# Where K and Q are rounded, when PSUM is evacuated, and which queue loads an index: eight edits to an attention and MLP kernel

## The chip, the core and the metric

The kernel runs on one core of a Trainium2 chip. The metric is device time in microseconds, as the median of several runs; one further execution was recorded by the hardware profiler. TensorE (PE), VectorE (DVE), ScalarE (ACT), GpSimd (POOL) and SyncE (SP) each take their own instructions in program order. DMAs are issued from SP, ACT or POOL.

## The reference

```python
# q, k, v: (8, 8, 576, 64) float32; global_idx: 8 positions
mask = (abs(i - j) <= 32) | is_global[i] | is_global[j]
attn = softmax(where(mask, q @ k.T / 8, -1e9))
x = (attn @ v) rearranged to (8 * 576, 512)
out = (s * relu(x @ w_in) ** 2 + b) @ w_out      # w_in 512x2048, w_out 2048x512
```

Every query sees a window of 32 positions on both sides and the 8 global positions. A global query sees all 576 keys.

## The kernel before, in words

**Pairs.** The 64 heads are worked as 32 pairs `p`, two heads at a time, four pairs to a batch (`bi, hp = divmod(p, 4)`). A pair has five chunks of 120 keys with the 8 global keys placed ahead of each, so that Q and K tiles have five blocks of 128 columns. For each chunk, `qk` (L482) makes one matmul into PSUM tile `pss` (pool `ps_s`, two buffers), ScalarE takes the exponential (`e`, L488) and VectorE multiplies by the mask (`em`, L491). In the next pair, `pv` (L501) multiplies by V and by ones into `po`. `norm_steps` (L519) then makes two ScalarE steps, `ln` (L541) and `rep` (L544), and VectorE writes the row `xt` (L547) of the MLP's input. `scatter` (L555) copies the results of global queries to their places in `xt`: eight GpSimd copies whose column is a register, `greg_p`, loaded at L808 from the index tile `gidx_i64`.

**Q and K of a pair.** Pairs 0 to 7 are loaded by GpSimd in bf16, six rows to a partition (`load_kq`, L152), and turned by TensorE transposes (`trans`, L437; `trans_a` for K, `trans_b` for Q). K is evacuated by VectorE (L457), Q by ScalarE for one head and then VectorE for the other (L473). Pairs from 8 on are loaded by SP in float32 (`load_nat`, L160) into rings `nat` of four, rounded to bf16 into `natb` of two (`round_nat`, L181), by ScalarE or, from p > 8 in pairs with hp 1 and 2, by GpSimd. K is then turned by a DMA transpose on SP (`turn_k`, L187), and Q by TensorE (`turn_q`, L193); VectorE places Q (L204). `put_kq` (L426) adds the global keys and queries by two small VectorE copies (L428, L432). V goes through a ring `vring` of four: `cast_v` rounds it on ScalarE (up to pair 7) or GpSimd, `put_v` (L419) adds the global values, by VectorE up to pair 7 and by a DMA on SP after that.

**MLP.** `moe_quanta` (L566) cuts the MLP into pieces of four TensorE matmuls: the first layer into `psh` (L581) with ReLU on ScalarE (`r`, L588) and the square on VectorE (`g`, L591); the second layer into `pso` (L596), then a VectorE evacuation (L607 or L610) and a store on SP. Evacuations of the first output rows wait for a bias row and are finished later by `release` (L840). From pair 5 on a pair has eight slots and takes about one quantum in each. By the order of the quanta, pairs with hp 1 and 2 carry the first layer and pairs with hp 3 and 0 the second.

**Order.** It is written by hand; the program is recorded in that order on each engine. `first_pair` (L708) runs slots 0 to 4 of pairs 0 to 4, without the MLP; `run_pair` (L640) runs slots 5 to 7 of pair 4 and all slots of the pairs after it. In a slot, the functions in `later` that the slot before left are run (`prev`), after the slot's own TensorE work; an evacuation that is appended to `later` so comes one slot after its matmuls:

```python
        for s in range(8) if p > 4 else range(NCH, 8):
            prev, later[:] = list(later), []
...
            for f in prev:
                f()
...
            for f in extra.get(s, ()):
                f()
            Q(nq[s])
```

A table `ex` (L868 to L902) gives each pair its extra work by slot: rounding at slots 5 and 7, `turn_k` and `put_v` at 7, `turn_q` at 5. Loads for pair `p + 4` are issued at the head of pair `p` (L856). A memset of eight elements (L855) at pair 5 lets SP start the loads of pair 8 only then.

Of the kernel before, what the change touches and what calls it, by code (L numbers as in the profile page):

```python
# [16 lines left out]
P = 128  # L17
# [49 lines left out]
def kernel(  # L67
# [45 lines left out]

    nat = {t: const.tile([P, NV, NCH, 2, D], FP32, name=f"nat{t}", tag=f"nat{t}") for t in "kq"}
    natb = {
        t: const.tile([P, 2, NCH * P], BF16, name=f"natb{t}", tag=f"natb{t}") for t in "kq"
    }

    xt = const.tile([P, 4, NX * S + 2 * HB * NCH - S], BF16)
# [16 lines left out]
            tensor=global_idx.tensor, offset=global_idx.offset, ap=[[0, P // NG], [1, NG], [1, 1]]  # L136
        ),
    )
    nc.sync.dma_start(out=gidx_i64[:], in_=_bcast_dram(global_idx[:], P))
    vring = const.tile([P, NV, NCH, 2, D], BF16)  # L140
    qbufs = [const.tile([P, 2, LQ], BF16, name=f"qbd{i}", tag=f"qbd{i}") for i in range(3)]
    gqd = [const.tile([P, 2, D], BF16, name=f"gqd{i}", tag=f"gqd{i}") for i in range(2)]
# [35 lines left out]

    kts = {}

    def round_nat(eng, t, p):  # L181
        eng(
            out=natb[t][0:KC, p % 2].rearrange("p (c h d) -> p c h d", c=NCH, h=2),
            in_=nat[t][0:KC, p % NV],
        )

    def turn_k(p):  # L187
        kts[p] = kqp.tile([P, KT0 + NCH * P], BF16, tag="kt", name="kt")
        nc.sync.dma_start_transpose(
            out=kts[p][:, KT0:].rearrange("p (c x) -> p c x", x=P), in_=natb["k"][:, p % 2]  # L190
        )

    def turn_q(p):  # L193
        ps = ps_s.tile([P, LQ], BF16, tag="s", name="pst")
        for c in range(NCH):
            nc.tensor.transpose(  # L196
                ps[:, P * c : P * c + P], natb["q"][:, p % 2, P * c : P * c + P], ident[:]
            )

        def place():  # L200
            ktile[p] = kts[p][:, KT0 - NG : KT0 - NG + LQ]
            for hh in range(2):
                r = slice(D * hh, D * hh + D)
                nc.vector.tensor_copy(  # L204
                    out=view(qbufs[p % 3][r, hh], [P, NCH], [HB + NG, 2], [1, HB]),
                    in_=view(ps[r], [P, NCH], [HB, 2], [1, HB]),
                )
            put_kq(p)

        later.append(place)  # L210

    def load_v(eng, p):
        load_nat(eng, "v", p)
# [221 lines left out]
        )  # L435

    def trans(t, p):  # L437
        if p < 5:
            ps = ps_m.tile([P, LQ], BF16, tag="moe", name="pst")
        else:  # L440
            ps = ps_s.tile([P, LQ], BF16, tag="s", name="pst")
        for j in range(NJ):
            n = N6 if j == NJ - 1 else NP6
            for hh in range(2):
                nc.tensor.transpose(
                    ps[D * hh : D * hh + D, NP6 * j : NP6 * j + n],
                    six[t][:n, p % NR, hh, j], ident[:n, :n],
                )
        return ps

    def trans_a(p, later=later):
        ps = trans("k", p)
        kt = ktp.tile([P, LQ], BF16, tag="kt", name="kt")
        ktile[p] = kt[:]

        def evac():
            nc.vector.tensor_copy(  # L457
                out=view(kt[:, NG:], [P, NCH], [NJ, KC // NJ], [1, NJ]),
                in_=view(ps[:], [KC // NJ, NCH], [1, KC // NJ], [NP6, NJ]),
            )  # L460
            if p >= 5:
                put_kq(p)

        later.append(evac)

    def trans_b(p, later=later):
        ps = trans("q", p)

        def evac():
            n = HB // NJ  # L470
            for hh, eng in ((1, nc.scalar.copy), (0, nc.vector.tensor_copy)):
                r = slice(D * hh, D * hh + D)
                eng(  # L473
                    out=view(qbufs[p % 3][r, hh], [P, NCH], [HB + NG, 2], [NJ, n], [1, NJ]),
                    in_=view(ps[r], [2 * n, NCH], [n, 2], [1, n], [NP6, NJ]),
                )
            if 1 < p < 5:
                put_kq(p)

        later.append(evac)  # L480

# [155 lines left out]

    A, V, G = nc.scalar.copy, nc.vector.tensor_copy, nc.gpsimd.tensor_copy

    def run_pair(p, nq, extra):  # L640

        bi, hp = divmod(p, 4)
        if hp == 0 and p > 4:
            open_batch(bi)
        for s in range(8) if p > 4 else range(NCH, 8):
            prev, later[:] = list(later), []
            if s < NCH:
                qk(p, s)
                if s in (1, 2):
                    step()  # L650
                if s == 4 and hp == 0 and bi > 1:
                    later.append(lambda: scatter(bi - 1))
                if s == 2 and p + 1 < NSIX:
                    cast_v(A, p + 1)
                if s == 2 and NSIX <= p + 2 < NPAIR:
                    cast_v(G, p + 2)
            elif s == 5:
                if p == 4:
                    cast_v(A, 5)
                if p + 1 < NSIX:  # L660
                    trans_b(p + 1)
            elif s == 6 and p + 1 < NSIX:
                trans_a(p + 1)
            for f in prev:
                f()
            if s == 0:
                pv(p - 1)
                pending.extend(norm_steps(p - 1))
            if s == 6 and p + 1 < NSIX:
                put_v(V, p + 1)  # L670
            for f in extra.get(s, ()):
                f()
            Q(nq[s])
# [34 lines left out]
    def first_pair(p, extra={}):  # L708
# [5 lines left out]
        for s in range(NCH):  # L714
            prev, later[:] = list(later), []
            now = []
            if p or s > 1:
                warm(1, bank)
            qk(p, s)
            if s in (1, 2):  # L720
                if p < 4:
                    (trans_a, trans_b)[s - 1](p + 1, now)
                if p:

                    pv(p - 1, (2 - s,))
                    if s == 1:
                        pending.extend(norm_steps(p - 1))
            elif s == 3:
                step()
            elif s == 4 and p == 3:  # L730
                cast_v(A, 4)
# [3 lines left out]
                f()  # L735
            if s == 1:
                step()
            if s == 0 and p == 4:
                put_v(V, 4)

# [12 lines left out]
    clear(qbufs[1][0:D, 1], LQ)  # L753
    clear(qbufs[1][D:P, 0], LQ)
    select_first()
    warm(3)
    vkey = const.tile([P, NCH], FP32)
    nc.vector.tensor_scalar(
# [20 lines left out]
    def clear_q2():  # L779
# [2 lines left out]

    first_pair(0, {
        1: [lambda: cast_v(A, 0), lambda: build_masks((2,)), steps0[0]],
        2: [steps0[1], lambda: build_masks((3, 4))],
        4: [clear_q2],
        3: [lambda: put_kq(1), steps0[2]],
    })
    for f in steps0[3:]:
        f()  # L790
# [6 lines left out]
    for p in (1, 2, 3, 4):  # L797
# [4 lines left out]
        elif p == 2:  # L802
            load_kq(6)
            load_v(nc.gpsimd, 6)
        elif p == 3:
            load_w_out(1)
            greg_p = [
# [11 lines left out]
    load_kq(7)  # L819
    load_v(nc.gpsimd, 7)  # L820
    load_w_out(3)
    onesf = const.tile([P, P], FP32)
    quanta[0] = 32

    def wpiece(j):
# [20 lines left out]
    for p in range(4, NPAIR):  # L846
# [6 lines left out]
        if p == 5:  # L853

            nc.vector.memset(nat["k"][0:1, 0, 0, 0, 0:8], 0.0)  # L855
        for j in {4: (), 5: (8, 9)}.get(p, (p + 4,)):  # L856
            for t in "kqv":
                if j < NPAIR:
                    load_nat(nc.sync, t, j)
# [2 lines left out]
        if p == 5:  # L862
            for i in range(NG):
# [1 line left out]
                    out=gvall[i : i + 1].rearrange("o (b h d) -> o b h d", b=B - 2, h=H),  # L865
                    in_=v[2:, :, ds(greg_p[i], 1), :].rearrange("b h o d -> o b h d"),
                )
        ex = {}  # L868

        def at(s, f, *a):  # L870
            ex.setdefault(s, []).append(lambda: f(*a))

        if p == 5:
            for t in natb.values():
                at(3, nc.vector.memset, t[96:P], 0.0)
            at(4, nc.vector.memset, onesf[:], 1.0)
        if p >= 6 and p + 2 < NPAIR:

            eng = G if p > 8 and hp in (1, 2) else A
            at(5, round_nat, eng, "k", p + 2)  # L880
            at(7, round_nat, eng, "q", p + 2)
            at(7, turn_k, p + 2)
            at(7, put_v, None, p + 2)
        if p % 8 > 4 and p + 3 < NPAIR:
# [3 lines left out]
            elif p % 8 == 6:  # L888
                at(1, steps[1])
        if p >= 7 and p + 1 < NPAIR:  # L890
            at(5, turn_q, p + 1)
        if 7 <= p < 15:
            for s in (4, 7):
                if adds:
# [3 lines left out]
        if p == 15:  # L898
            assert not adds
            at(2, bias)  # L900
        if p > 15 and held_rows:
            at(4, release)  # L902
        run_pair(p, nq, ex)
    flush()
    pv(NPAIR - 1)
    pending.extend(norm_steps(NPAIR - 1))
# [40 lines left out]
```

## Time and profile before

| | |
|---|---|
| median of 7 runs | 374.19 us (373.92 to 375.85) |
| profiled execution | 373.85 us, of which the span from first to last instruction is 372.2 us |
| busy in the span | PE 346.7, DVE 241.8, ACT 216.4, POOL 96.1 us |
| mean granted TensorE clock | 0.97 |

In the profile, a row of a timeline gives start and duration in us, engine, line, operation, the tiles written and read, and in brackets the idle time before it and what ended it. A row of the waits gives who waited for whom, the total in us, how often, and the longest. A row of a table by stretches gives the stretch, its length, then busy us (and number of instructions) of PE, weight loads, DVE, ACT and POOL, the granted clock, the DMA share and GB/s. The page cuts the span into 40 slices and shows each engine's busy tenths, and the granted clock in tenths (`PEclk`). A row of the chain of waits gives start, duration and what the time went to; `POOLq` is GpSimd's sequencer, `issue` is time without a wait that the profile knows.

### The profile page before, as it was taken

How to read it: one execution, taken by the hardware profiler on the slowest of the kernel's cores; microseconds unless marked ns; L12 is line 12 of the kernel's file. 1: busy time of each engine (PE TensorE's matmuls, PEld its weight loads, DVE VectorE, ACT ScalarE, POOL GpSimd, SP SyncE). 2: the span in 40 equal slices, each digit the busy share in tenths (PEclk: the TensorE clock that was granted, in tenths of full speed). 3: DMA queues.
4: the chain of work that ended last, by engine and by line, in shares of the span. 5: the costliest groups of instructions: out<-in, count | busy, mean ns of one | idle time of the engine just before them, and what ended most of it. 6: DMA issues, size and time to landing. Idle time of an engine off the chain costs nothing.

```text
span 372.2 us, 7693 instructions
## 1 busy us (share of the span) xinstructions
PE 346.7 (93%) x2740; PEld 180.8 (49%) x2740; DVE 241.8 (65%) x633; ACT 216.4 (58%) x417; POOL 96.1 (26%) x185
## 2 busy tenths in 40 slices
PE   5688698799999989999999899999999999999995
PEld 2254244355445545557755445545557744444442
DVE  4867548569886999577767786676666734522421
ACT  7468467755775567458755775577557742611710
POOL 7954473115223620051204200320040001000000
PEclk9579889999999999999999999999999999999999
DMA  6999599998896893577778668695521002002002
GB/s 130 210 208 212 96 193 223 187 178 191 170 211 169 182 178 82 120 181 172 153 177 203 168 141 189 161 190 105 133 77 50 2 37 77 2 28 85 2 29 85
DMA packets 125638, 50.10 MB, mean 135 GB/s; under 512 B 113320, under 2 KB 118440, under 8 KB 125600
## 3 DMA queue, kind: packets, MB, share of 16 engines
q1 hardware_dynamic: 116848, 37.30, 47.1%
q0 software_dynamic: 8544, 12.03, 15.8%
q8 instruction: 21, 0.34, 0.4%
q10 hardware_dynamic: 208, 0.29, 0.3%
q14 instruction: 17, 0.14, 0.1%
HBM read 42.26 MB, written 9.44 MB: 139 GB/s over the span
## 4 chain that ended last, share of the span: by engine, by line
PE 63%; DVE 19%; ACT 6%; issue 6%; DMA 2%; POOLq 1%; POOL 1%; SPq 0%; ACTq 0%; DVEq 0%
PE pso L596 30%; PE psh L581 18%; PE po L510 7%; PE pss L484 5%; DVE g L591 4%; DVE em L491 3%; DVE xt L547 2%; DVE qbd L204 2%; ACT r L588 2%; DMA gidx_i<-in_global_idx_dram 2%; ACT e L488 2%; ACT ln L541 1%; PE pst L196 1%; DVE kt L428 1%; POOLq L808 1%
## 5 line engine op out<-in xcount | busy, mean ns | idle before, releaser
L581 PE MATMUL psh<-xt,win_t 128*128 128x512 bf16 (+2 forms) x704 | 141.1, 345 | 2.6 <-POOL xt L558 2.6
L596 PE MATMUL pso<-wout_t,g 128*128 128x512 bf16 x576 | 137.1, 379 | 0.0
L588 ACT ACTIVATE r<-psh 128x512 bf16<-128x512 f32 x144 | 88.8, 616 | 60.6 <-PE psh L581 58.4
L488 ACT ACTIVATE e<-pss 128x384 bf16<-128x384 f32 (+1 forms) x160 | 76.6, 481 | 66.7 <-PE pss L484 65.8
L581 PEld LDWEIGHTS <-win_t 128*128 128x128 bf16 x704 | 64.3, 99 | 57.5 <-issue 5.4
L591 DVE TENSOR_TENSOR g<-r 128x512 bf16<-128x512 bf16 x144 | 62.6, 443 | 42.4 <-ACT r L588 42.3
L596 PEld LDWEIGHTS <-g 128*128 128x128 bf16 x576 | 54.8, 98 | 60.8 <-issue 0.6
L491 DVE TENSOR_TENSOR em<-e,mask 128x384 bf16<-128x384 bf16 (+1 forms) x160 | 61.9, 390 | 32.2 <-ACT e L488 31.9
L484 PE MATMUL pss<-qbd,kt 128*128 128x384 bf16 (+1 forms) x160 | 51.8, 325 | 10.0 <-DVE qbd L432 8.3
L610 DVE SCALAR_TENSOR_TENSOR osb<-pso,s_bc,bias_row 128x512 f32<-128x512 f32 x28 | 21.0, 748 | 34.1 <-PE pso L596 34.0
L558 POOL COPY xt<-xg 128x4 bf16 x64 | 15.4, 241 | 102.8 <-DVE xt L547 99.3
L216 POOL CAST vring<-natv 128x640 bf16<-128x640 f32 x27 | 21.4, 795 | 53.3 <-PE po L510 46.4
L484 PEld LDWEIGHTS <-kt 128*128 128x128 bf16 x160 | 15.8, 99 | 31.1 <-DVE kt L428 7.9
L541 ACT ACTIVATE ln<-po 128x640 f32<-128x640 f32 x32 | 22.5, 704 | 6.3 <-PE po L510 6.3
L547 DVE TENSOR_TENSOR xt<-po,rep 128x600 bf16<-128x600 f32 x32 | 24.9, 778 | 1.6 <-ACT rep L544 1.2
L544 ACT ACTIVATE rep<-ln 128x640 f32<-128x640 f32 x32 | 23.8, 745 | 0.0
L204 DVE COPY qbd<-pst 64x600 bf16<-64x600 bf16 x48 | 22.3, 464 | 0.6 <-PE pst L196 0.2
L510 PE MATMUL po<-em,vring 128*64 128x160 bf16 (+3 forms) x448 | 19.8, 225 | 0.4 <-ACT ln L541 0.4
L510 PEld LDWEIGHTS <-vring 128*64 128x64 bf16 x448 | 15.8, 111 | 8.6 <-issue 6.8
L510 PE MATMUL po<-em,onesb 128*64 128x160 bf16 (+2 forms) x448 | 19.2, 222 | 0.6 <-DVE xt L547 0.5
L706 PE MATMUL psw<-dummy 128*128 128x512 bf16 x34 | 15.0, 498 | 1.3 <-DVE dummy L228 1.3
L510 PEld LDWEIGHTS <-onesb 128*64 128x64 bf16 x448 | 15.0, 113 | 1.5 <-DVE xt L547 1.1
(107 smaller groups left out, 217.8 us busy)
## 6 DMA issues: line engine op xcount, KB each, us to landing
natv<-in_v_dram SPq DMA_DIRECT2D x55, 150.0 KB, 4.7
out_dram<-osb SPq DMA_DIRECT2D x28, 256.0 KB, 2.0
natk<-in_k_dram SPq DMA_DIRECT2D x47, 150.0 KB, 3.0
natq<-in_q_dram SPq DMA_DIRECT2D x47, 150.0 KB, 3.4
wst<-in_moe_w_out_dram POOLq DMA_DIRECT2D x8, 512.0 KB, 5.9
win_t<-in_moe_w_in_dram POOLq DMA_DIRECT2D x2, 1024.0 KB, 13.2
wout_t<-in_moe_w_out_dram POOLq DMA_DIRECT2D x4, 512.0 KB, 8.6
out_dram<-osbh SPq DMA_DIRECT2D x8, 256.0 KB, 2.2
```

The costliest lines, as they stand in the source:

```text
L204: nc.vector.tensor_copy(out=view(qbufs[p % 3][r, hh], [P, NCH], [HB + NG, 2], [1, HB]), in_=view(ps[r], [P, NCH], [HB, 2], [1, HB]),)
L484: nc.tensor.matmul(ps[:], ktile[p][:, P * c : P * c + P], qbufs[p % 3][:, :, LO[c] : HI[c]])
L488: nc.scalar.activation(e[:], ps[:], AF.Exp, scale=SCALE)
L491: later.append(lambda: nc.vector.tensor_mul(em[:], e[:], masks[c]))
L510: nc.tensor.matmul(po[D * hh : D * hh + D, a : a + n], onesb[:] if part else vring[:, p % NV, c, hh], emt[(p, c)][:, hh, x : x + n], start ...
L541: nc.scalar.activation(ln[:], po[:, LQ : 2 * LQ], AF.Ln)
L544: nc.scalar.activation(rep[:], ln[:], AF.Exp, scale=-1.0)
L547: lambda: nc.vector.tensor_tensor(out=view(xt[:, hp, x0:], [KC, NCH], [HB, 2], [1, HB]), in0=halves(po[:, 0:LQ]), in1=halves(rep[:]), op=O ...
L581: nc.tensor.matmul(psh[:, d0 : d0 + n], win_t[:, a, f * P : f * P + P], xt[:, a, x0 : x0 + n], start=(a == 0 and j == 0), stop=(a == 3), s ...
L588: nc.scalar.activation(r[:], psh[:], AF.Relu)
L591: later.append(lambda g=g, r=r: nc.vector.tensor_mul(g[:], r[:], r[:]))
L596: nc.tensor.matmul(pso[:], gl[f][:, u * P : u * P + P], wout_t[:, f], start=(f == 0), stop=(f == 15),)
```

## The change

1. `natb` holds four pairs instead of two. All rounding is ScalarE's, and it is done only in pairs with hp 0 and 3: pair with hp 0 rounds `p + 3` (slots 5, 7) and `p + 4` (slots 1, 3), pair with hp 3 rounds `p + 2` and `p + 3`. Pair 6 rounds pair 8.
2. Float32 loads come one pair earlier (`p + 5`); pair 7 loads 11 and 12.
3. `turn_q`, and `trans_a` and `trans_b` of pairs 6 and 7, put their evacuation into `now`, which is run ahead of `prev` in the same slot.
4. In `first_pair` the next pair is turned at slots 0 (Q) and 1 (K) instead of 1 (K) and 2 (Q); pair 5 at slots 3 and 4 of pair 4, out of pool `ps_m`. Pair 4 makes both normalization steps of pair 3 in slot 1. Steps of the first batch's globals in pair 0 move by a slot.
5. `flush` follows `select_first` at once, so that the global keys and queries of pair 0 are placed ahead of the mask preparations.
6. The index tile `gidx_i64` is loaded from ScalarE's queue instead of SP's.
7. The memsets of `natb`'s last partitions and of `onesf` move from VectorE in pair 5 to GpSimd after pair 2.
8. `put_v` of pairs 5 to 7 is a DMA on SP instead of a VectorE copy. The eight releases come two to a pair, at slots 2 and 6, in pairs with hp 0 and 3 from pair 16 on.

```diff
-        t: const.tile([P, 2, NCH * P], BF16, name=f"natb{t}", tag=f"natb{t}") for t in "kq"
+        t: const.tile([P, NV, NCH * P], BF16, name=f"natb{t}", tag=f"natb{t}") for t in "kq"
...
-    nc.sync.dma_start(out=gidx_i64[:], in_=_bcast_dram(global_idx[:], P))
+    nc.scalar.dma_start(out=gidx_i64[:], in_=_bcast_dram(global_idx[:], P))
...
-        if p < 5:
+        if p < 6:
             ps = ps_m.tile([P, LQ], BF16, tag="moe", name="pst")
...
-            if p >= 5:
+            if p > 1:
                 put_kq(p)
...
-                if p + 1 < NSIX:
-                    trans_b(p + 1)
-            elif s == 6 and p + 1 < NSIX:
-                trans_a(p + 1)
-            for f in prev:
+                if 4 < p < NSIX - 1:
+                    trans_b(p + 1, now)
+                elif turn:
+                    turn_q(turn, now)
+            elif s == 6 and 4 < p < NSIX - 1:
+                trans_a(p + 1, now)
+            for f in now + prev:
                 f()
...
             if s == 6 and p + 1 < NSIX:
-                put_v(V, p + 1)
+                put_v(None, p + 1)
...
+            if p == 4 and s > 2 or p < 4 and s < 2:
+                (trans_b, trans_a)[1 - s % 2 if p == 4 else s](p + 1, now)
...
             if s == 1:
                 step()
+                if p == 4:
+                    step()
...
     select_first()
+    flush()
     warm(3)
...
             load_v(nc.gpsimd, 6)
+            for t in natb.values():
+                nc.gpsimd.memset(t[96:P], 0.0)
+            onesf = const.tile([P, P], FP32)
+            nc.gpsimd.memset(onesf[:], 1.0)
         elif p == 3:
...
-        for j in {4: (), 5: (8, 9)}.get(p, (p + 4,)):
+        for j in {4: (), 5: (8, 9), 6: (10,), 7: (11, 12)}.get(p, (p + 5,)):
...
-            eng = G if p > 8 and hp in (1, 2) else A
-            at(5, round_nat, eng, "k", p + 2)
-            at(7, round_nat, eng, "q", p + 2)
+            todo = {0: (p + 3, p + 4), 3: (p + 2, p + 3)}.get(hp, (8,) if p == 6 else ())
+            for i, j in enumerate(todo):
+                if j < NPAIR:
+                    at(5 - 4 * i, round_nat, "k", j)
+                    at(7 - 4 * i, round_nat, "q", j)
             at(7, turn_k, p + 2)
...
-        if p > 15 and held_rows:
-            at(4, release)
+        if p > 15 and hp in (0, 3) and held_rows:
+            at(2, release)
+            at(6, release)
```

## The prediction

> **What bounds the kernel now.** I read the engine shares and slices first, then a table of two stretches, the waits, and the timelines where a wait is long.
>
> ```profile
> PE   5688698799999989999999899999999999999995
> ...
> PEclk9579889999999999999999999999999999999999
> ```
>
> ```profile
> 0.00:80.00 80.00, 62.86 (x614) 30.87 (x614) 53.34 (x164) 52.25 (x97) 42.63 (x77) 0.87 1.00 180
> 80.00:372.00 292.00, 283.86 (x2129) 149.96 (x2128) 188.49 (x470) 164.15 (x320) 53.49 (x108) 1.00 0.54 122
> ```
>
> From 80 us on TensorE is busy 283.86 of 292 us, so only its gaps can be won there. Before that it idles 17.1 us, its clock is halved twice, and the DMA engines are full (share 1.00). Which gaps, the waits say:
>
> ```profile
> PE pss L484 <- DVE qbd L432: 8.3, 11, 1.8
> ...
> PE psh L581 <- POOL xt L558: 2.6, 1, 2.6
> ...
> DVE gidx_f L742 <- DMA gidx_i<-in_global_idx_dram: 2.0, 1, 2.0
> ```
>
> The 8.3 us are starts of pairs that wait for Q and K on VectorE: in the waits cut at 80 us, 4.2 us in 7 waits lie after, 4.1 in 4 before (1.55 us ahead of pair 6, 1.84 ahead of pair 7). The longest one after 80 us, at 136.59, in the timeline:
>
> ```profile
> 127.03 2.64 DVE L491 TENSOR_TENSOR em<-e,mask 128x320 bf16<-128x320 bf16 x1
> ...
> 127.36 0.73 POOL L216 CAST vring<-natv 128x640 bf16<-128x640 f32 x1
> ...
> 128.02 0.73 POOL L182 CAST natbk<-natk 120x640 bf16<-120x640 f32 x1
> ...
> 128.68 0.72 POOL L182 CAST natbq<-natq 120x640 bf16<-120x640 f32 x1
> ...
> 136.59 0.30 PE L484 MATMUL pss<-qbd,kt 128*128 128x320 bf16 x1 [1.27 <-DVE qbd L432]
> ```
>
> A 0.33 us mask product took 2.64 us while GpSimd cast without pause, and VectorE stayed late to the end of the pair. The other place is the start of the MoE, in the chain:
>
> ```profile
> 39.25 0.15 POOLq L808
> 39.48 0.05 POOLq L558
> 39.53 2.21 issue
> 41.74 0.04 POOLq L558
> 41.78 0.21 POOL xt L558
> ```
>
> GpSimd's sequencer loads eight index registers (L808, 34.1 to 39.4), prepares the first scatter copy at 39.48, and then does nothing, not even the next register operation, until that copy's wait ends at 41.74. A waiting instruction holds this sequencer. Eight copies follow (2.08 us); the first MoE matmul starts at 43.89.
>
> **What the Trainium skill says.** *SBUF — State Buffer*, "Who interferes with whom": a VectorE instruction with two SBUF inputs is blocked by a GpSimd instruction that reads SBUF, not by one that only writes. The 2.64 us agree for the first half; no run shows the second. *VectorE: DVE Perf Modes*, "Zero memsets can be issued as uint32": a memset costs a cycle per element whatever the type, and VectorE packs zeros. The trace agrees: the packed 32x640 memsets (L871) took 0.592 us. *Perfetto Trace Analysis*, "GPSIMD Engine Instruction": spans of GpSimd instructions are unreliable, spacing is better. *TensorE: Matmul & The Clock Gate*, Part 1: an idle window halves the clock. Here 2.6 us idle before 43.89 go with a half clock to about 50 us (the first 12 `psh` take 5.28 us, later four take 0.86).
>
> **The change, part by part**, against the profiled execution (373.85 us; span 372.2), which is 0.34 below the median 374.19.
>
> *Index load on ScalarE's queue; `flush` after `select_first`; first pairs turned a slot earlier.* VectorE's wait for the index (2.0 us) can shrink by all of it, the 1 us of small operations between `qbd` and the first Q/K placement go behind it, and the starts of pairs 2, 3 and 4 lose their stalls (0.62, 0.38, 0.38). About 3 us by pair 4. Both scaling steps of pair 3 move to slot 1 of pair 4, so its `xt` is ready near 37 instead of 41.7. The issue (0.58 us) moves from SP, whose V loads start earlier, to ScalarE ahead of its table load, where ScalarE later waits 0.44 for Q. All this counts only if the scatter can start sooner; it cannot, as follows.
>
> *Memsets of `natb` and `onesf` to GpSimd after pair 2.* In the built order they stand between the V load of pair 6 (ends 35.0 in GpSimd's timeline) and L358 with the index loads. They are not packed: 32x2560 each. The trace has memsets of 128x192 at 0.26, of 8x128 at 0.19 and of 128x8 at 0.09 us: 0.84 to 0.9 ns an element, so 2.15 us each, 4.3 for both; by spacing (two of 8x128 stand 0.14 ahead of their successor) it is at most 1.1 ns, 2.8 us each. `onesf` waits for the second to end, and by the chain above that holds the sequencer with the index loads behind it. The earlier V loads may pull the DMA stream ahead by 0.5. Sum: 34.5 + 4.3 + 0.1 = 38.9; loads 5.4 (34.08 to 39.48): 44.3; copies 2.1: first MoE matmul near 46.4, **2.5 us later**. Bounds: with packed-like 0.6 us each, 0.7 earlier; at 2.8 each, 3.8 later. I take 2.5. The half clock after it stays as it is: TensorE idles even longer. VectorE is rid of 1.35 us in pair 5.
>
> *Pairs 5 and 6: evacuations lead, `put_v` by DMA.* Before, VectorE's row at the end of pair 6 is `qbd` 69.18, `g` 69.88, `vring` 70.21 (0.47), `kt` 70.61, placements to 71.55. Now `qbd` waits only for ScalarE's half, which stands ahead of a 0.77 cast: 67.3 + 0.65 = 67.95. Then `qbd` 0.78, `em` 0.32, `g` 0.42, `kt` 0.77, placements 0.3: 70.45 against 71.55, **1.1 won**. The same sum for pair 5 (ScalarE's half ends 56.85) gives 59.3 for 60.2: **0.9 won**. VectorE now stands up to 1 us before ScalarE's half, with ready `em` and `g` behind it; that is in the sums. Three 0.72 us DMA issues join SP, which is held by full DMA engines then.
>
> *Rounding on ScalarE only.* 22 casts of 0.76 us leave GpSimd. ScalarE gets 22 of 0.72, four per second-layer pair instead of two: 1.4 us more in a 9.2 us pair where it is busy 5 to 6 tenths. In pair 8 a cast behind `ln` delays `exp(2)` to about 84.5; qk(4) needs it at 84.8, so nothing. Covered in the steady pairs. VectorE is no longer blocked in first-layer pairs except by one V cast and the scatter.
>
> *`turn_q` places in slot 5.* One `em` and one `g` (0.75 us) no longer stand ahead. The gaps at 174.6 and 212.5 (0.74, 1.14) also follow a release (L842: 1.20 and 0.68 us) that leaves these pairs. I take the 4.2 us after 80 to shrink to 0.3: **3.9 won**. `place` now needs K's turned tile a slot earlier; it is issued about a pair ahead, so nothing in the steady state.
>
> *Four deep, loads a pair earlier.* At pair 7 two pairs (11, 12) are loaded back to back, with pair 9's K transpose behind them on SP. The trace issued pair 11 from 74.98 to 80.58; a second 3 to 5 us puts K of 12 near 84. ScalarE rounds it in slot 1 of pair 8: 79.75 less the 2.0 won, plus 3.5, = 81.3. It stands there, `exp(2)` behind it, and qk(4) behind that. Bounds: 0 if the DMA engines run freer, 3.3 with the transpose late too. I take **1.6 lost**.
>
> *Releases* (0.68 us each, 8 as before) go two to a second-layer pair, where VectorE is busy 6 to 9 tenths: nothing, or 0.7 a pair without that cover.
>
> Sum: +2.5 − 0.9 − 1.1 − 3.9 + 1.6 = −1.8: 372.05 for such an execution, 372.4 as a median.
>
> **Rivals.** (1) *The memsets are cheap or do not hold the index loads*: 0.7 won instead of 2.5 lost, 369.2. For it: unreliable GpSimd spans. Against: the idle sequencer in the chain. (2) *It cancels*: V casts and scatters still block VectorE (the `em` at 127.03 was held by a V cast first), and 2.5 instead of 3.9 us are won: 373.8. (3) *Slower: the load queue.* The DMA share is 1.0 to 1.2 up to 80 us, and the double load is one more pair in it. If K of 12 comes at 85 and the transposes of 9 and 10 late behind it, ScalarE stands 3.7 and VectorE 1.8 us in line: 5.5 instead of 1.6, 376.3. It decides above 4.5 us. Against it: SP catches up 3 us a pair.
>
> **Numbers.** About 0.3% (1.1 us) is what a measurement of this kernel can tell from no change. Forecast 0.33; rival 1 0.15; no change 0.22; slower 0.30, most of it rival 3, the rest memsets near 2.8 us with it. So faster 0.48, same 0.22, slower 0.30. The range runs from rival 1 (369.0) to rival 3 (376.5). The forecast's own range is 371 to 373.
>
> **What would show it.** Right: two long memsets on GpSimd near 35 to 39, L808's successor after 39, the first `psh` near 46; no TensorE gap over 0.3 us at ends of first-layer pairs; a wait of ScalarE's rounding for `natk` in pair 8. Wrong: `psh` before 43.5 (rival 1), gaps still at the first-layer pairs' ends (rival 2), TensorE idle over 4 us between 78 and 95 (rival 3).

## The result, and the profile after

The changed kernel takes 377.88 us (median of 23 runs, 375.94 to 379.81) against 374.73 for the kernel before (60 runs), a ratio of 1.0087 with a 95% interval of 1.0073 to 1.0101: **slower by 3.2 us**, where 372.4 was forecast. The profiled execution took 377.71 us, with a span of 376.1 against 372.2. (The MoE in what follows is the MLP; its first matmul is the first that writes `psh`.)

The page after, TensorE and its granted clock in 40 slices:

```profile
PE   5788389895999999999999999999999999999995
...
PEclk9669769998899999999999999999999999999999
```

A slice is 9.4 us. Two places have got worse: the fifth slice (38 to 47 us), where TensorE is busy for 3 tenths, 6 before, and the tenth (85 to 94), where it is half idle, with the clock at 8 in it and in the next. Before, the tenth was full. From the twelfth slice on the two kernels differ by a tenth at most.

The table of two stretches, after (length; PE busy, PEld, DVE, ACT, POOL, each with its instructions; clock, DMA share, GB/s):

```profile
0.00:80.00 80.00, 60.42 (x600) 29.59 (x601) 49.04 (x151) 52.16 (x98) 45.59 (x78) 0.85 0.96 171
80.00:376.00 296.00, 287.77 (x2144) 151.91 (x2141) 185.79 (x477) 175.68 (x343) 41.68 (x88) 0.99 0.56 123
```

The rounding has gone where it was sent: in sum 12 us left GpSimd in the second stretch (53.49 before) and came to ScalarE (164.15 before).

The waits after (who waits, for whom: sum, times, longest):

```profile
PE psh L579 <- POOL xt L556: 7.6, 1, 7.6
...
ACT natbk L182 <- DMA natk<-in_k_dram: 4.6, 1, 4.6
...
PE pss L482 <- ACT e L486: 4.4, 2, 4.0
PE pss L482 <- DVE qbd L432: 4.0, 4, 2.6
```

The waits for `qbd`, 8.3 us in 11 before, are 4.0 in 4. The start of the MoE has grown from 2.6 to 7.6, and there is a new chain: ScalarE waits 4.6 us for a load of K, and TensorE 4.0 for ScalarE.

Where the time went is read most easily from the first `pss` matmul of each pair in the two timelines:

| stretch | before | after | difference | forecast |
|---|---|---|---|---|
| start to first `psh` | 43.89 | 48.81 | +4.92 | +2.5 |
| to start of pair 6 | 16.31 | 14.62 | -1.69 | -0.9 |
| pair 6 to 7 | 11.39 | 10.09 | -1.30 | -1.1 |
| pair 7 to 8 | 8.16 | 9.43 | +1.27 | 0 |
| pair 8 to 9 | 9.02 | 15.71 | +6.69 | +1.6 |
| pair 9 to 31 | 207.52 | 201.16 | -6.36 | -3.9 |
| pair 31 to the end | 75.91 | 76.24 | +0.33 | 0 |
| span | 372.20 | 376.06 | +3.86 | -1.8 |

So the change won more in its long part than forecast, and lost it again, and more, in two places of the first 100 us. Each column is one execution. The stretch from pair 9 to 31 can be relied on: in four of the kernels below (a1, a2, b4, e1) that leave this part of the changed kernel as it is, it took 201.15 to 201.17. The start is less steady, as will be seen.

**First loss.** GpSimd's timeline after (start, length, what):

```profile
33.07 0.69 POOL L155 DMA_DIRECT2D sixk<-in_k_dram  x1 [4.04 <-PE pst L445]
...
36.85 2.23 POOL L810 MEMSET natbk<- 32x2560 bf16 x1
39.02 2.23 POOL L810 MEMSET natbq<- 32x2560 bf16 x1
41.30 0.21 POOL L812 MEMSET onesf<- 128x128 f32 x1
...
46.72 2.04 POOL L556 COPY xt<-xg 128x4 bf16 x8 [4.40 <-issue]
```

The two memsets are as long as forecast. The idle time of 4.40 us is that of the sequencer's eight index loads, which run from 41.53 to 46.5 in the chain. What the forecast missed is in the first line: the load of pair 6's K, and all behind it, stands at 33.07, where it stood at 31.31 before. (The releaser in the bracket is inferred, and wrong, as will be seen.) Without the memsets these 1.8 us would hardly show, as an estimate: before, the index loads were done 2.2 us before the scatter could start.

**Second loss.** The timeline of pair 8 after, SyncE's queue, ScalarE and TensorE:

```profile
84.47 3.71 SPq L171 DMA_DIRECT2D natk<-in_k_dram  x2
...
91.05 0.72 ACT L182 CAST natbk<-natk 120x640 bf16<-120x640 f32 x1 [4.58 <-DMA natk<-in_k_dram]
91.69 0.48 ACT L486 ACTIVATE e<-pss 128x384 bf16<-128x384 f32 x1
...
92.22 0.42 PE L482 MATMUL pss<-qbd,kt 128*128 128x320 bf16 x1 [3.95 <-ACT e L486]
```

The rounding of pair 12's K stands on ScalarE ahead of `exp(2)` of pair 8, and waits for a load whose issue ends at 88.2. TensorE idles 3.95 us, and the clock record is halved from 90.65 to 97.48, which costs another 2.7 (6.69 less 3.95; half of the 5.3 us from 92.22 to 97.48 is 2.6).

**The gain.** From the start of pair 9 to 368.5 before, and to 372 after, one row of the table each:

```profile
88.77:368.50 279.73, 275.09 (x2060) 145.31 (x2058) 181.56 (x454) 159.49 (x311) 51.35 (x100) 1.00 0.53 121
```

```profile
98.66:372.00 273.34, 273.29 (x2060) 145.31 (x2058) 175.43 (x453) 168.59 (x329) 37.25 (x77) 1.00 0.54 120
```

The same 2060 matmuls; TensorE idles 4.6 us before and nothing after. Busy time is 1.8 lower too: each start of a pair that had waited cost some 0.16 us more than the gap that the trace shows (pair 13 to 14 is 1.42 shorter, its gap was 1.27; pair 17 to 18 0.91, gap 0.74). There were eleven such starts, the seven that the prediction counts and four with gaps of 0.07 to 0.11: their gaps sum to 4.56 us, and eleven times 0.16 is 1.8, which together make the 6.36. A cast of V on GpSimd still holds a mask product, but away from the end of a pair:

```profile
136.50 1.91 DVE L489 TENSOR_TENSOR em<-e,mask 128x320 bf16<-128x320 bf16 x1
136.84 1.39 POOL L216 CAST vring<-natv 128x640 bf16<-128x640 f32 x2
```

The pair after it starts at 144.18 without a wait.

### The profile page after: what moved, and what is told of

Read it like the earlier page. It is cut to its first block, busy times and chain, and to the rows that moved or that the text cites. A ratio compares the mean times of both kernels' runs of the same rounds, so it can differ in the third digit from the quotient of the medians.

```text
span 376.1 us, 7674 instructions
## 1 busy us (share of the span) xinstructions
PE 348.2 (93%) x2740; PEld 181.5 (48%) x2740; DVE 234.8 (62%) x627; ACT 227.8 (61%) x439; POOL 87.3 (23%) x166
## 3 DMA queue, kind: packets, MB, share of 16 engines
q0 software_dynamic: 8544, 12.03, 15.8%
## 4 chain that ended last, share of the span: by engine, by line
PE 80%; DMA 6%; POOL 3%; ACT 3%; issue 2%; SPq 2%; DVE 2%; POOLq 1%; ACTq 0%
PE psh L579 32%; PE pso L594 31%; PE po L508 8%; PE pss L482 6%; PE pst L196 2%; DMA gidx_p<-in_global_idx_dram 2%; SPq L171 2%; DMA vring<-gvx 2%; DMA natk<-in_k_dram 1%; DMA gf<-in_v_dram,grow 1%; ACT e L486 1%; POOLq L816 1%; DVE kt L428 1%; PE psw L707 1%; POOL natbk L810 1%
## 5 line engine op out<-in xcount | busy, mean ns | idle before, releaser
L594 PE MATMUL pso<-wout_t,g 128*128 128x512 bf16 x576 | 139.4, 384 | 0.0
L589 DVE TENSOR_TENSOR g<-r 128x512 bf16<-128x512 bf16 x144 | 59.0, 424 | 49.7 <-ACT r L586 49.3
L489 DVE TENSOR_TENSOR em<-e,mask 128x384 bf16<-128x384 bf16 (+1 forms) x160 | 60.6, 380 | 38.3 <-ACT e L486 38.3
L216 POOL CAST vring<-natv 128x640 bf16<-128x640 f32 x27 | 24.1, 910 | 71.6 <-PE po L508 62.4
L556 POOL COPY xt<-xg 128x4 bf16 x64 | 14.6, 229 | 108.2 <-DVE xt L545 100.3
L182 ACT CAST natbk<-natk 120x640 bf16<-120x640 f32 x24 | 17.6, 735 | 4.6 <-DMA natk<-in_k_dram 4.6
L182 ACT CAST natbq<-natq 120x640 bf16<-120x640 f32 x24 | 17.9, 745 | 0.0
## 6 DMA issues: line engine op xcount, KB each, us to landing
win_t<-in_moe_w_in_dram POOLq DMA_DIRECT2D x2, 1024.0 KB, 15.8
wout_t<-in_moe_w_out_dram POOLq DMA_DIRECT2D x4, 512.0 KB, 10.2
```

What stands on the lines that cost most here:

```text
L182: nc.scalar.copy(out=natb[t][0:KC, p % NV].rearrange("p (c h d) -> p c h d", c=NCH, h=2), in_=nat[t][0:KC, p % NV],)
L216: eng(out=vring[:, p % NV], in_=natv[:, p % NV])
L489: later.append(lambda: nc.vector.tensor_mul(em[:], e[:], masks[c]))
L589: later.append(lambda g=g, r=r: nc.vector.tensor_mul(g[:], r[:], r[:]))
L594: nc.tensor.matmul(pso[:], gl[f][:, u * P : u * P + P], wout_t[:, f], start=(f == 0), stop=(f == 15),)
```

## The experiments

Each ratio is to the kernel before, beside it on the same chip, with its 95% interval. Places and gaps are those of one profiled execution each.

**Is it the wait of `onesf`? (a1)**

```diff
-            for t in natb.values():
-                nc.gpsimd.memset(t[96:P], 0.0)
             onesf = const.tile([P, P], FP32)
             nc.gpsimd.memset(onesf[:], 1.0)
+            for t in natb.values():
+                nc.gpsimd.memset(t[96:P], 0.0)
```

> The changed kernel with one edit: onesf is cleared ahead of the two natb tiles, so that it has no earlier GpSimd instruction to wait for. Theory (the wait of onesf for the end of the second natb memset holds GpSimd's sequencer, and with it the eight index loads of 5.05 us): the loads start near 37.1 beside the memsets (4.5 us, to 41.5) and end near 42.1, the eight scatter copies near 44.3; first psh at 44.4 instead of 48.8, and the time 4.4 us shorter, 373.5. Rival (the memsets themselves stand in line, the index loads go after them whatever the last one waits for): first psh stays at 48.8, time 377.9.

373.16 us, ratio 0.9947 (0.9926 to 0.9968); first `psh` 45.13. The theory held. GpSimd's timeline of this kernel:

```profile
37.29 0.22 POOL L810 MEMSET onesf<- 128x128 f32 x1
37.56 2.23 POOL L812 MEMSET natbk<- 32x2560 bf16 x1
...
42.99 2.09 POOL L556 COPY xt<-xg 128x4 bf16 x8 [0.30 <-issue]
```

The index loads ran from 37.79 to 42.49, beside the memsets. The order of three lines is worth 4.7 us, median against median, and 3.7 us at the first `psh`: what held the loads was one waiting instruction, not the memsets' work.

**Memsets off GpSimd (a2).** Back on VectorE in pair 5 (`at(3, nc.vector.memset, t[96:P], 0.0)` and `at(4, nc.vector.memset, onesf[:], 1.0)`).

> The changed kernel with the three memsets back on VectorE in pair 5 (slots 3 and 4), as before the change, though natb is twice as long. Theory (memsets ahead of the index loads cost the start of the MoE): index loads from about 36 to 41.2, copies to 43.4, first psh at 43.5, 5.3 us earlier; VectorE takes about 2.5 us more in pair 5, of which up to 1 us shows at the start of pair 6: 372.6 to 373.6. Rival (the start is late because GpSimd's loads of pair 6 begin 1.8 us later than before, not because of the memsets): first psh near 47, time 376.

372.03 us, ratio 0.9944 (0.9914 to 0.9974); first `psh` 43.21, pair 6 behind a gap of 2.16 us in place of 0.60. The theory held, though the gap grew by 1.56 where up to 1 was expected. In pair 8 TensorE still waited 4.50 us for the rounding, with the first of SyncE's loads of K at 45.57 instead of 51.82: the second loss doesn't come from the late start.

**Which load? (a3)** In pair 8, pair 11 is rounded in slots 1 and 3 and pair 12 in 5 and 7:

```diff
+            if p == 8:
+                todo = todo[::-1]
             for i, j in enumerate(todo):
```

> The changed kernel with one edit: in pair 8 ScalarE rounds pair 11 in slots 1 and 3 and pair 12 in slots 5 and 7, not the other way round. Theory (the 3.95 us gap of TensorE at 88.27 is ScalarE's rounding of K of pair 12 in slot 1, which waits for a load that lands at 91, and the half clock of 90.65 to 97.48 follows from it): K of pair 11 is there, the gap and about 2.8 us of half clock go: 6.7 us less, 371.2. Rival (the whole load queue is late, so K of pair 11 isn't there either, or the wait only moves to slot 5): 2 us or less is won, 376 or more.

374.42 us, ratio 1.0000 (0.9979 to 1.0020). The time lies between theory and rival: in the profiled execution (376.90 us, above the median) the gap in pair 8 went, and a new one of 2.66 us came at the start of pair 9, with half a clock again. The timeline there:

```profile
90.89 1.22 SPq L189 DMA_TRANSPOSE kt<-natbk  x1
...
94.62 0.18 DVE L428 COPY kt<-gkt 128x40 bf16<-128x40 bf16 x1 [2.76 <-DMA kt<-natbk]
```

This is K of pair 9, whose transpose stands on SyncE behind the loads of pairs 11 and 12. The wait for K of pair 12 had hidden a second one.

**Both edits (a4).**

> Both of the two edits before: memsets on VectorE in pair 5, and pair 8 rounds pair 11 first. Theory (the two losses are separate and everything after pair 9 is 6.4 us faster than before): 5 and 6.7 us less, 366.2, that is 8.5 us under the kernel before. Rival (one loss covers the other, since an earlier MoE start also moves TensorE's pair 8 earlier against the load queue): 2 to 3 us less than the better of the two alone, 369 or more.

369.83 us, ratio 0.9878 (0.9830 to 0.9925): the rival, the losses are not separate in full. A gap of 2.20 us stays ahead of pair 9 (K of pair 9 again), and 2.16 ahead of pair 6.

**Is it only the order on SyncE? (c1)** Memsets on VectorE, pair 12 loaded behind the transpose of pair 9, and rounded in slots 5 and 7 of pair 9:

```diff
-        for j in {4: (), 5: (8, 9), 6: (10,), 7: (11, 12)}.get(p, (p + 5,)):
+        for j in {4: (), 5: (8, 9), 6: (10,), 7: (11,)}.get(p, (p + 5,)):
...
             at(7, turn_k, p + 2)
             at(7, put_v, None, p + 2)
+            if p == 7:
+                for t in "kqv":
+                    at(7, load_nat, nc.sync, t, 12)
```

> Memsets on VectorE as in the second run, and pair 12 taken out of the double load: its loads go into SyncE's queue in slot 7 of pair 7, behind the transpose of K of pair 9, and ScalarE rounds it in slots 5 and 7 of pair 9 instead of 1 and 3 of pair 8. Theory (after the swap TensorE waited 2.2 to 2.7 us for K of pair 9, whose transpose stood behind the loads of pairs 11 and 12 on SyncE; the double load costs both this and the wait for K of pair 12): no gap over 1 us between pairs 7 and 10, no half clock there, 4.5 + 1.7 us less than with the memsets alone (372.03): 365.9. Rival (the DMA engines are full and the same bytes have to come in any case): a wait of 2 us or more stays at the start of pair 9 or 10, 368.5 or more.

371.07 us, ratio 0.9898 (0.9856 to 0.9941). The theory fell, the rival held. In the profiled execution (373.21 us, the longest of four) pair 9 starts without a wait, but pairs 10 and 11 then wait 2.24 and 3.04 us for their K. In the waits of 75 to 130 us of this kernel:

```profile
DVE kt L428 <- DMA kt<-natbk: 6.0, 2, 3.4
```

The loads of one pair, six of 150 KB, are 0.9 MB; at the 171 GB/s of the table above that is, as an estimate, about 5 us of full DMA engines; the DMA share is 1.18 from 78 to 130 us here. Bringing the bytes forward moved the wait and didn't remove it. That the order on SyncE plays no part isn't shown: here the loads of pairs 12 and 13 stand back to back (82.93 to 91.16) ahead of the transpose of pair 10's K, and no kernel issued the transposes from another queue.

**The extra depth only from pair 15 on (d1).** Memsets on VectorE; until pair 15 loads four pairs ahead and two roundings in slots 5 and 7 of every pair, on ScalarE:

```diff
-        for j in {4: (), 5: (8, 9), 6: (10,), 7: (11, 12)}.get(p, (p + 5,)):
+        for j in {4: (), 5: (8, 9), 15: (19, 20)}.get(p, (p + 4 + (p > 15),)):
...
-            todo = {0: (p + 3, p + 4), 3: (p + 2, p + 3)}.get(hp, (8,) if p == 6 else ())
+            todo = {0: (p + 3, p + 4), 3: (p + 2, p + 3)}.get(hp, ())
+            if p < 15:
+                todo = (p + 2,)
```

> Memsets on VectorE in pair 5, and the fourth pair of depth only from pair 15 on: until then each pair loads four pairs ahead as before the change and ScalarE rounds two pairs ahead in slots 5 and 7; pair 15 loads 19 and 20, and from there it is the changed kernel. Theory (moving a pair of loads forward costs time only while the DMA engines are full, which ends near 145 us): no TensorE gap over 1 us between 75 us and the end, and 4.5 + 1.7 us less than with the memsets alone (372.03): 365.9. Rival (what was lost around pairs 8 to 12 isn't the extra depth but the later start of the loads, or the rounding in first-layer pairs costs as much): 369 or more.

367.96 us, ratio 0.9806 (0.9725 to 0.9888). The stretch in which the changed kernel lost most, here:

```profile
78.00:130.00 52.00, 52.00 (x411) 26.80 (x410) 42.20 (x102) 33.52 (x68) 15.69 (x31) 1.00 0.96 191
```

52.00 of 52.00 us busy: the theory's picture. The DMA share of the stretch doesn't tell the two kernels apart (0.96 here, 0.94 in the changed kernel, where TensorE is busy 47.82). The time is 2 us above its number. In the profiled execution (369.16 us) the MoE started at 46.32, 3.1 us later than in a2, for a reason that comes next; what the other three executions did isn't on record. And pairs 9 to 31 take 201.04 us, as in the changed kernel (201.16): up to pair 15 the depth and the choice of pairs for the rounding won nothing. The edit takes back both at once, the earlier loads and the rounding that needs them earlier; which of the two costs isn't separated.

**Why GpSimd is 1.8 us late (b4, e1).** A first idea was that K of the next pair is now turned a slot later than Q, so that its buffer comes free later. K first again, `[1 - s % 2 if p == 4 else 1 - s]` for `[1 - s % 2 if p == 4 else s]`:

> The changed kernel, but in pairs 0 to 3 K of the next pair is turned in slot 0 and Q in slot 1 (the change had made it Q first). Theory (1.8 us of the 4.9 us by which the MoE starts later come from here: GpSimd's load of pair 6's K waits until K of pair 3 is turned, at 32.53 instead of 30.78, and the memsets and index loads stand behind it): the load starts 1.1 us earlier, first psh at 47.7 instead of 48.8, time 376.8. Rival (GpSimd waits for something else there): first psh stays at 48.8, time 377.9.

377.43 us, ratio 1.0062 (1.0039 to 1.0084), the load at 33.93, first `psh` 49.54: the theory fell. The traces show another order of causes. In the built program each DMA of GpSimd waits for the one eight before it, and for the load of pair 6's K that is the second load of `win_t`. In the fourteen kernels that don't put other work ahead of it, GpSimd's wait there ended 0.02 to 0.03 us after that load had landed (30.75 and 30.78 before, 32.51 and 32.53 after). And `win_t` is issued 1.8 us later (16.69 for 14.89) because the gathers ahead of it are. VectorE and GpSimd, before:

```profile
5.94 0.15 DVE L276 CAST gpf<-gidx_p 128x1 f32<-128x1 int32 x1 [0.16 <-DMA gidx_p<-in_global_idx_dram]
...
6.62 1.11 POOL L293 DMA_INDIRECT gf<-in_k_dram,grow  x1 [0.28 <-DVE grow L279]
```

and after:

```profile
7.79 0.15 DVE L276 CAST gpf<-gidx_p 128x1 f32<-128x1 int32 x1 [2.36 <-DMA gidx_p<-in_global_idx_dram]
...
8.42 1.11 POOL L293 DMA_INDIRECT gf<-in_k_dram,grow  x1 [1.82 <-DVE gidx_f L745]
```

Both loads of the index are issued at 1.34 now, on two queues, and both are used near 8: `gidx_i` gains 0.2 us (8.27 to 8.05), `gidx_p` loses 1.85. This is what the Trainium skill lets one expect: *DMA: Bandwidth & Descriptors*, "Queues, rings and completion order", says that each DMA engine takes packets in turn from the queues that have work for it, so a second queue shares the engines and adds none. In all thirteen kernels with the load on ScalarE's queue the gathers start between 8.18 and 8.94; in the four with both loads on SyncE's they start at 6.62 to 6.65, and once at 7.94. The step from the issue of `win_t` to its landing is loose, however: 14.15 to 18.09 us in these seventeen executions. The landing came at 31.31 to 35.17 with the load on ScalarE's queue (mean 32.7), at 30.36 to 32.42 on SyncE's (mean 31.1). That is 1.6 us in the mean, but one execution can hide it: in b6 below `win_t` is issued at 14.92, as before the change, and lands at 32.42, as after it. The load back on SyncE:

> The changed kernel with the index load (gidx_i) back on SyncE's queue, behind gidx_p. Theory (with both on their way at once gidx_p lands 1.8 us later, at 7.8 instead of 5.9; the gathers on GpSimd wait for it, and the whole queue behind them: the second win_t lands 1.8 us later and the load of pair 6's K waits for that landing): gathers start at 6.6 instead of 8.4, second win_t lands near 30.8, first psh at 47.0 instead of 48.8, time 376.1. Rival (the DMA engines are full by then, and the landing of win_t doesn't follow its issue): first psh stays near 48.8, time 377.9 or more, since pair 0 starts up to 1 us later.

376.24 us, ratio 1.0040 (1.0012 to 1.0067): the time is the theory's 376.1, and the interval lies below that of the changed kernel. The way there isn't: `win_t` landed at 30.36 and pair 6's K was loaded at 30.91, though the gathers started at 7.94 in this execution. First `psh` was only 0.4 us earlier, at 48.45: with the selection of pair 0 late again (its first `pss` at 12.79, 2.3 us later), `xt` of pair 3 was ready only at 45.63, and the scatter waited 0.65 us for that and its eight copies took 2.70 us for 2.04. In this execution the edit shortens one chain and lengthens the other, and pairs 7 and 8 are shorter (by 3.1 us in sum) and what lies between the first `psh` and pair 7 longer (by 2.2).

**Where the gain comes from (b6, b1, b2, b3).** The kernel before with one edit, `eng = A` for every pair in `round_nat`'s call:

> The kernel before with one edit: the rounding of K and Q goes to ScalarE in every pair, in the places it had (slots 5 and 7), so GpSimd has no rounding. Theory (GpSimd's casts that block VectorE make most of the 4.4 us of gaps after pair 9): the gaps shrink to the two behind a release (1.9 us) or less, 2.5 to 4 us faster, 371.7. Rival (1.4 us more of ScalarE's time in first-layer pairs delays its 0.62 us relu steps, and TensorE waits for them instead): no gain, 374.6 or more.

372.44 us, ratio 0.9940 (0.9914 to 0.9965): 2.2 us won, a little under the theory's 2.5 to 4. Its waits from 80 us on, where the kernel before had 4.2 in 7:

```profile
PE pss L484 <- DVE qbd L432: 1.8, 6, 0.6
```

The rounding back on GpSimd in the changed kernel (pairs from 11 on, still in second-layer pairs only):

> The changed kernel, rounding of pairs 11 and later on GpSimd, still in the second layer's pairs. From pair 9 on the changed kernel has no gap on TensorE and takes 6.4 us less than the one before. Theory (what cost time was that the casts stood in the first layer's pairs, at whose ends VectorE is late): up to 0.5 us more, 378.2. Rival (any cast on GpSimd that blocks VectorE costs, in whatever pair): 2 to 4 us of gaps come back, 380 or more.

378.31 us, ratio 1.0092 (1.0062 to 1.0122): no difference from the changed kernel that the medians can tell, as the theory has it. Only its time is used here, since the profiled execution took 382.62 us. Its times spread more, from 375.66 to 383.05, so that a cost in some executions isn't excluded. In second-layer pairs GpSimd's casts of K and Q cost nothing that the median shows; in first-layer pairs, in the kernel before, they cost the 2.2 us of b6. That the pairs alone make this difference isn't shown, since b1 places the turned Q earlier as well.

The placing of the turned Q behind the slot before, from pair 8 on, `(now if p < 9 else later).append(place)`:

> The changed kernel, but from pair 8 on the placing of the turned Q goes behind the work of the slot before, one slot later, as it did before the change. Theory (the lead is part of the gain): 0.2 to 0.4 us are lost at the ends of most of the 12 first-layer pairs, 3 us in all, 380.9. Rival (with the casts gone from these pairs VectorE has slack at their ends and the order doesn't matter): no change, 377.9.

380.80 us, ratio 1.0187 (1.0133 to 1.0240): 2.9 us more than the changed kernel, the theory. In the profiled execution pairs 9 to 31 took 2.0 us longer; another 0.9 stands ahead of pair 9, where the MoE started 0.9 later (first `psh` at 49.69), which the edit doesn't touch. From 98 us on gaps of 0.25 us came back at the ends of three first-layer pairs; the waits of this kernel there:

```profile
PE pss L482 <- DVE qbd L432: 0.9, 4, 0.3
```

The releases as before, one in slot 4 of each pair from 16 on:

> The changed kernel with the releases as before the change: one in slot 4 of each pair from 16 on, so in first-layer pairs too. Theory (each release there, 0.7 to 1.2 us of VectorE ahead of the pair's end, makes part of the gaps at the ends of pairs 17, 18, 21 and 22): gaps of 0.3 to 0.6 us come back there, 1.5 us more, 379.4. Rival (with no cast on GpSimd in these pairs VectorE has slack enough): no change, 377.9.

376.86 us, ratio 1.0052 (1.0027 to 1.0078), no wait for `qbd` from 98 us on. The rival: no loss. With the casts gone and Q placed earlier, VectorE has room for a release in these pairs.

**A version that beats both (d2, d3, e4).** Memsets and index loads on GpSimd ahead of the V load of pair 5 and of the K load of pair 6, and the late depth of d1:

```diff
     load_kq(5)
+    onesf = const.tile([P, P], FP32)
+    nc.gpsimd.memset(onesf[:], 1.0)
+    for t in natb.values():
+        nc.gpsimd.memset(t[96:P], 0.0)
...
             load_w_out(0)
+            greg_p = [
+                nc.gpsimd.value_load(g32[:1, i, 0:1], min_val=0, max_val=S - 1)
+                for i in range(NG)
+            ]
```

> As the run before, but the three memsets stand on GpSimd ahead of the V load of pair 5 (where GpSimd waited 3 us), and the eight index loads behind that pair's loads, ahead of the K load of pair 6. Theory (the MoE starts when its last input is there; with memsets and index loads out of the way this is xt of pair 3, or TensorE's own work until 41.2): first psh near 41.5, no memset in VectorE's pair 5 (1.5 us of the 2.16 us gap ahead of pair 6 go): 1.8 + 1.5 us less than the run before, 362.6. Rival (the loads behind these on GpSimd come up to 5 us later, and TensorE waits for K or V of pairs 5 and 6 instead): 366 or more.

368.50 us, ratio 0.9822 (0.9750 to 0.9893): the rival held. First `psh` was at 43.41, since the scatter waited for `xt` until 40.73, and in pair 7 a new wait stood:

```profile
70.38 1.01 PE L508 MATMUL po<-em,vring 128*64 128x160 bf16 x14 [3.19 <-DMA vring<-gvx]
```

It is the DMA that places V rows of pair 7, issued at 63.37 among loads; in the changed kernel the same wait is 0.80 us, at 73.83. The half clock that follows it here lasts 6.8 us. VectorE places them again, `put_v(V, p + 1)`:

> As d2_all_early, but the V rows of the global keys of pairs 6 and 7 are placed by VectorE, as before the change, not by a DMA of SyncE. Theory (the 3.19 us gap at 67.19 is that DMA, issued at 63.4 among loads that fill the DMA engines, landing near 70.3; half a clock of 6.8 us follows it): the gap goes and VectorE pays 0.47 us at the ends of pairs 5 and 6: 368.5 - 3.2 - 1.7 + 0.9 = 364.5. Rival (the loads are late by then whatever is in front of them, and the wait moves to K, Q or V of pair 8): 367 or more.

365.19 us, ratio 0.9776 (0.9709 to 0.9843): the theory held. And with the index load back on SyncE:

> As the run before, with the index load back on SyncE's queue as well. Theory (the memsets and index loads no longer stand in the way, and the MoE then starts when xt of pair 3 is ready, near 40.8, so GpSimd's queue being 1.8 us earlier gives nothing, and the later selection of pair 0 costs up to 0.5 us): 364.5 to 365. Rival (GpSimd's queue still sets the pace of the first 60 us, its loads 1.8 us earlier): 1 to 2 us less than the run before.

364.72 us, ratio **0.9748 (0.9688 to 0.9809)**, the fastest, 13 us under the changed kernel. Its difference to the run before it (364.85 to 367.51 there, 363.97 to 365.32 here, four runs each) isn't settled by these. A part of what these versions win may be luck: no half clock follows the start of the MoE in the profiled executions of d2, d3 and e4, while in the kernel before 5.9 us of work after it ran at half clock, about 3 us lost.

## Why the prediction was wrong

- **Gaps after 80 us, 3.9 won: right in kind, too small.** They went, and 6.36 us with them from pair 9 on. The term left out the 0.16 us that a wait costs beside its gap, 1.8 us in eleven waits, and the shortest gaps. The rounding alone gives 2.5 us of it (pairs 9 to 31: 205.03 against 207.52), the lead of Q's placing 2.0 when it is taken from the changed kernel; the releases and, up to pair 15, the depth added nothing. The release that the forecast saw at the gaps of 174.6 and 212.5 wasn't needed for them: b3 has it and no gap.
- **Pairs 5 and 6, 0.9 and 1.1 won: right.** The gap ahead of pair 6 went from 1.55 to 0.60, that ahead of pair 7 from 1.84 to 0.59. (Of the 1.69 us in the table some 0.8 more, an estimate, are the half clock, which covered 5.9 us of work after the first `psh` before and 4.3 after.) But the V rows by DMA, for which the forecast only counted three issues on SyncE, gave back 0.80 in pair 7.
- **Memsets, 2.5 lost: the mechanism was right, its start was not.** Their length (2.23 us, forecast 2.15) and the hold of the sequencer are as forecast; a1 shows the hold. The failed term is "34.5": the memsets started at 36.85, because pair 6's loads ahead of them waited for `win_t`. A part of this, 1.6 us in the mean of the executions above, lies in the edit that the forecast counted as a gain: "VectorE's wait for the index (2.0 us) can shrink by all of it". The index was used only 0.2 us earlier, and the other index load, ahead of the gathers on GpSimd's queue, came 1.85 later. The step looked at who waits for the load that moved, not at the load whose place it shares. How much of the 1.8 us in this one execution is the edit and how much the scatter of the landing stays open.
- **Four deep, 1.6 lost: this step failed most**, with 6.69. It forecast K of pair 12 "near 84" and put the 5.5 us of the same mechanism to a rival with a threshold of 4.5 us. The wait of ScalarE was forecast as 2.7 us (84 less 81.3) with 1.6 left on TensorE; it was 4.58, with 3.95 left. Two terms were too small. The forecast gave K of pair 12 "3 to 5 us" after the issue of pair 11's loads, which is what the issue took (84.47 to 88.18); the data was there only when the cast began at 91.05, 2.9 us after the issue and 6.6 after pair 11's loads. The page before had 3.0 us from issue to landing for such a load. And the half clock behind the gap, 2.7 us, wasn't in the sum. The forecast's timing of pair 8 against the loads was nearly right, though it left out on both sides that the MoE starts later: pair 11's loads began 2.8 us ahead of pair 8 in the sum and 3.0 in the trace. a3 and c1 show that the wait moves when one load moves, and d1 that it goes when the 0.9 MB are not brought forward in this stretch; that full DMA engines are the reason is argued from their share in this stretch (0.94 in the changed kernel, 1.18 in c1); the queue's order as the reason isn't excluded.
- **The rivals.** The slower one (376.3) named the right queue and the late transposes of pairs 9 and 10 behind it. It left out the memsets' late start, and so lay 1.6 us under the result; that its total came so near is in part luck, since the long part won 2.5 us more than either had. It added the two waits up; in the traces one hides behind the other, and K of pair 9 showed only when pair 12 was out of the way.

Open: whether the fourth pair of depth and the rounding in second-layer pairs only are of any use after pair 15; no kernel was run without them there that had the lead of Q's placing. And the parts of the gain overlap, so 2.5 and 2.0 aren't shares of one sum.

## What to carry to other kernels

Before loads are brought forward a step, see whether the DMA engines and the queue have room in that stretch: with the share near 1.0 here, moving the loads within the queue only moved the wait (a3, c1). In a sum of when a load is there, count its landing and not only its issue. Of a load that is moved to another queue, look also at what was in flight at that time, and at all that waits for it. An initialisation that is put on another engine is judged by what it waits for and what stands behind it: three memsets cost 4.7 us more in one order than in another. And a landing that scatters by 2 us from one execution to the next can't be read from one profile of each kernel.

## What was not expected of the hardware

- Two loads of the eight indices to 128 partitions, issued 0.75 us apart on one queue, were used at 5.94 and 8.27; issued together on two queues, at 7.79 and 8.05. The earlier one was used at 7.55 to 8.30 in all thirteen kernels with two queues, at 5.80 to 5.94 in three of the four with one, and at 7.31 in e1.
- A DMA issued on GpSimd waits, as this program is built, for the landing of the DMA eight before it: an early 1 MB load (15.8 us from issue to landing) held a small one for 4 us.
- While the two memsets ran on GpSimd (36.85 to 41.25), VectorE's mask products took as long as elsewhere (0.32 us at 37.31, two in 0.67 at 37.95); beside casts that read SBUF one took 2.64 before and 1.91 after. So a run does show the second half of what the prediction says no run shows, that an instruction on GpSimd that only writes doesn't hold VectorE.
- A gap of 2.60 us ahead of the first `psh` went with half a clock in the kernel before, where the first matmuls after it start 427 ns apart; in a4, c1, d2, d3 and e4 gaps of 2.63 or 2.64 us at the same place didn't, and they start 215 ns apart. The Trainium skill, *TensorE: Matmul & The Clock Gate*, Part 1, has windows of about 3.4 us that run free of the kernel; the half clocks here last a multiple of 3.4 us (3.4, 6.8, 10.2 and once 13.7 us between 40 us and the last one, which the end of the kernel cuts off), which agrees, and so a gap shorter than a window may or may not cost one. In pair 8, too, the length is chance: 6.8 us behind the 3.95 us in the changed kernel, 3.4 behind 4.50 in a2. A mean clock is to be checked against the matmuls: e4's record begins only at 24.17, its table says 1.00 from the start, and its warm-up matmuls up to 9 us are 427 ns apart all the same.
